# Sliding-window halo by VectorE, dilated v by a casting load: one change to an attention and feed-forward kernel

## The chip, the cores and the metric

The kernel runs on one core of a Trainium2 chip. The metric is the device time in microseconds (us), and less is better. The kernel before takes 308.5 us, the median of three runs (307.8 to 308.51). The profile comes from one further execution, with a span of 307.1 us.

Names used below: PE is TensorE (matrix multiplies), PEld its weight loads, DVE is VectorE, ACT is ScalarE, POOL is GpSimd, SP is SyncE, which here only issues DMA transfers. `Lnnn` is a line of the kernel file.

## The reference

The attention output is laid out token by token and goes through a feed-forward part with a squared ReLU.

```python
# q, k, v: (8 rows of the batch, 8 heads, 576 tokens, 64), float32
window, dilation = 32, 4
rel = pos[:, None] - pos[None, :]
mask_plain = (rel >= 0) & (rel < window)                                        # heads 0 to 3: sliding
mask_dil = (rel >= 0) & (rel < window * dilation) & (rel % dilation == 0)       # heads 4 to 7: dilated
scores = where(mask, q @ k.T / sqrt(64), -1e9)
attn_out = softmax(scores) @ v

x = attn_out.transpose(0, 2, 1, 3).reshape(4608, 512)
out = square(relu(x @ w_in)) @ w_out          # w_in (512, 2048), w_out (2048, 512)
```

## The kernel before

The program goes through the eight batch rows. In row b it issues the attention of row b and, between its pieces, the matmuls of feed-forward chunk b - 1 (512 tokens). The call `pump(n)` issues the next n pieces of that chunk, so that PE always has matmuls between the attention's steps. [...]

For the sliding heads the 576 tokens are cut into six blocks of 96 queries. A block needs the 32 keys before it too, so each block of `vp` has 128 partitions: partitions 32 to 127 hold the block's own 96 tokens, and partitions 0 to 31 the last 32 of the block before. The copy of those 32 partitions (the halo) is what `halo_sliding_by_dma` does. Dilated v has a halo of the same kind, 64 partitions of `vd`.

```python
QB = 96; NB = S // QB; PADP = P - QB          # 96, 6, 32
vp = [const.tile([P, NB, HH, D + 2], FP16, name=f"vp{r}") for r in range(2)]
vd = [const.tile([P, 2, DIL, HH, D + 2], FP16, name=f"vd{r}") for r in range(2)]
sv = stg.tile([P, HH, NB, D], FP32, name="sv")          # staging of sliding v
sd = stg.tile([P, 2, HH, DIL * D], FP32, name="sd")     # staging of dilated v
# ...
def load_sliding_qk(b):                                  # casting loads, issued by GpSimd
    n = natp.tile([P, HH, 9 * D], FP16, name=f"ns{b}", tag="n")
    for i, s in ((1, k), (0, q)):
        nc.gpsimd.dma_start(out=n[64 * i : 64 * (i + 1)], in_=s[b, 0:HH].rearrange(...))
    return n

def load_dilated_v(b, eng):
    vv = v[b, HH:H].rearrange("h (i c) d -> i h (c d)", c=DIL)
    for t in range(2):
        eng.dma_start(out=sd[P - QD[t] : P, t, :, :], in_=vv[Q0D[t] : Q0D[t] + QD[t]])

def cast_sliding_v(b, ms=range(0, NB, 2)):               # 3 casts on GpSimd
    for m in ms:
        nc.gpsimd.tensor_copy(vp[b % 2][:, m : m + 2, :, 0:D], sv[:, :, m : m + 2, :].rearrange(...))

def cast_dilated_v(b):                                   # 4 casts on GpSimd
    for t in range(2):
        p0 = 64 * t
        for c in range(0, DIL, 2):
            nc.gpsimd.tensor_copy(vd[b % 2][p0:P, t, c : c + 2, :, 0:D], sd[p0:P, t, :, D * c : D * (c + 2)].rearrange(...))

def halo_sliding_by_dma(b):
    nc.sync.dma_start(out=vp[b % 2][0:PADP, 1:NB], in_=vp[b % 2][P - PADP : P, 0 : NB - 1])

def halo_dilated_by_dma(b):
    nc.sync.dma_start(out=vd[b % 2][0:64, 1], in_=vd[b % 2][64:P, 0])
# ...
def after_transposes(b):          # GpSimd waits here until the transposes of row b have landed
    nc.gpsimd.tensor_copy(seen, QKTd[b % 2][:, 0, 1, KPAD : KPAD + 1])
# ...
def attn_values_by_dma(b, then):
    xs = x_tiles(b)
    for mp in range(3):
        av_sliding(b, mp, xs)     # matmuls of pav from vp, then rcp_p and xs on VectorE
        if mp == 1:
            then[0]()
        pump(3)
    x_sliding_by_dma(b, xs)       # xT <- xs, DMA transposes
    ys = []
    for t in range(2):
        for a in range(2):
            av_dilated(b, t, a, xs)            # matmuls of paw from vd, then rcp_d and xd on VectorE
            pump(4 + 2 * (a > t))
        ys.append(x_dilated_by_dma(b, t, xs))  # yd <- xd, DMA transpose
        then[1 + t](ys[t])
    pump(6)
    x_from(b, 0, ys[0])                        # xT <- yd on ScalarE
    pump(7)
    x_from(b, 1, ys[1])
# ...
for b in range(4, B):
    pending.append(moe_gen(b - 1))
    nxt = b + 1
    if nxt < B:
        after_transposes(b)
        ns = load_sliding_qk(nxt)
        dd = keep_dilated_qk(nxt)              # q and k of the dilated heads to DRAM as fp16, by GpSimd
    if b > 4:
        cast_dilated_v(b)
    halo_sliding_by_dma(b)
    halo_dilated_by_dma(b)
    dps = []

    def copied():
        if nxt < B:
            dps.append(turn(nxt, ns))          # nr <- ns on VectorE (token order), dp <- nr by SyncE
    def first(y):
        if nxt < B:
            load_sliding_v(nxt)
    def second(y):
        if nxt < B:
            transpose_sliding(nxt, dps[0])     # QKTp <- dp
            transpose_dilated(nxt, dd)         # QKTd <- dd
            load_dilated_v(nxt, nc.sync)       # sd <- v
            nc.gpsimd.tensor_copy(seen, y[:, 0, 0, 0:1])
            cast_sliding_v(nxt)

    pump(3)
    attn_scores(b, 3)
    attn_values_by_dma(b, (copied, first, second))
    pump(1000)
```

The feed-forward chunk ends with seven block products; near the end, `pa` holds the sixth product, `pb` the seventh, and VectorE adds them to the output tiles `ou` and `ov`:

```python
        yield from product(A, sq(1), wq(1, 1))
        take(upper, 1)                                   # ScalarE copies pa
        leave(upper, 0, (1,) if last else (0, 1))        # output store
        yield
        yield from product(Bk, gq(1, 1), tq(3))
        add(o21, Bk)                                     # VectorE: ov
```

Of the kernel before, what the change touches and what calls it, by code (L numbers as in the profile page):

```python
# [8 lines left out]
FP16 = mybir.dt.float16  # L9
# [4 lines left out]
P = 128  # L14
# [3 lines left out]
def kernel(  # L18
# [9 lines left out]
    nc = tc.nc  # L28

    B, H, S, D = q.shape  # L30
    W = 32
    DIL = 4
# [3 lines left out]
    HH = H // 2  # L36
# [10 lines left out]
    NB = S // QB  # L47
    PADP = P - QB
# [41 lines left out]
    vp = [const.tile([P, NB, HH, D + 2], FP16, name=f"vp{r}") for r in range(2)]  # L90
    vd = [const.tile([P, 2, DIL, HH, D + 2], FP16, name=f"vd{r}") for r in range(2)]
    sv = stg.tile([P, HH, NB, D], FP32, name="sv")
    sd = stg.tile([P, 2, HH, DIL * D], FP32, name="sd")
    ident = const.tile([P, P], FP16, name="ident")
    maskp = const.tile([P, UW], FP16, name="maskp")
    maskd = const.tile([P, UW], FP16, name="maskd")
# [12 lines left out]
    def load_sliding_qk(b):  # L109
        n = natp.tile([P, HH, 9 * D], FP16, name=f"ns{b}", tag="n")  # L110
        for i, s in ((1, k), (0, q)):
            nc.gpsimd.dma_start(
                out=n[64 * i : 64 * (i + 1)],
                in_=s[b, 0:HH].rearrange("h (p j) d -> p h (j d)", j=9),
            )
        return n
# [14 lines left out]
            for h in (0, 2):  # L131
                nc.sync.dma_start(out=sv[PADP:P, h : h + 2], in_=vv[:, h : h + 2])  # L132

    def load_dilated_v(b, eng):
        vv = v[b, HH:H].rearrange("h (i c) d -> i h (c d)", c=DIL)
        for t in range(2):
            eng.dma_start(out=sd[P - QD[t] : P, t, :, :], in_=vv[Q0D[t] : Q0D[t] + QD[t]])  # L137
# [29 lines left out]
    def cast_sliding_v(b, ms=range(0, NB, 2)):  # L167
        for m in ms:
            nc.gpsimd.tensor_copy(  # L169
                vp[b % 2][:, m : m + 2, :, 0:D], sv[:, :, m : m + 2, :].rearrange("p h m d -> p m h d")  # L170
            )

    def cast_dilated_v(b):
        for t in range(2):
            p0 = 64 * t
            for c in range(0, DIL, 2):
                nc.gpsimd.tensor_copy(  # L177
                    vd[b % 2][p0:P, t, c : c + 2, :, 0:D],
                    sd[p0:P, t, :, D * c : D * (c + 2)].rearrange("p h (c d) -> p c h d", d=D),
                )  # L180
# [7 lines left out]
    def halo_dilated(b, c):  # L188
        nc.scalar.copy(
            vd[b % 2][0:64, 1, c : c + 2, :, 0:D], vd[b % 2][64:P, 0, c : c + 2, :, 0:D]  # L190
        )

    def halo_sliding_by_dma(b):
        nc.sync.dma_start(out=vp[b % 2][0:PADP, 1:NB], in_=vp[b % 2][P - PADP : P, 0 : NB - 1])
# [9 lines left out]
    def keep_dilated_qk(b):  # L204
        d = dpool.tile([2, HH * CL, DIL * D], FP16, name=f"dd{b}", tag="dd")
        for i, src in ((1, k), (0, q)):
            nc.gpsimd.dma_start(
                out=d[i].rearrange("(r i) x -> r (i x)", i=4),
                in_=src[b, HH:H].rearrange("h (r i) d -> (h r) (i d)", i=16),
                max_dma_last_dim=4096,  # L210
            )
        return d
# [21 lines left out]
    def after_transposes(b):  # L234
        nc.gpsimd.tensor_copy(seen, QKTd[b % 2][:, 0, 1, KPAD : KPAD + 1])
# [117 lines left out]
    def mm2_strassen_gen(c, g):  # L353
        A, Bk, Ck = "abc"
        banks = {}

        def wq(r, q):
            return lambda k: wo[2 * r + k // 4][:, k % 4, HM * q : HM * (q + 1)]

        def gq(i, r):  # L360
            return lambda k, t: g[:, HF * r + k, HTOK * i + P * t : HTOK * i + P * (t + 1)]

        def tq(n):
            return lambda k: wt[n][:, k]

        def sq(n):
            return lambda k, t: gs[n][:, k, P * t : P * (t + 1)]

        def product(bank, a, b, ts=(0, 1)):
            new = bank not in banks  # L370
            if new:
                banks[bank] = pmool.tile([P, 2, HM], FP32, name=f"p{bank}{c}", tag="pm")
            for t in ts:
                for k in range(HF):
                    nc.tensor.matmul(  # L375
                        banks[bank][:, t],
                        a(k, t),
                        b(k),
                        start=(new and t == 0 and k == 0),
                        stop=(k == HF - 1),  # L380
                        skip_group_check=True,
                    )
                    if k % 4 == 3 and (t, k) != (ts[-1], HF - 1):
                        yield

        def half(i):
            return otp.tile([P, 2, DM], FP32, name=f"o{i}_{c}", tag="ot")

        def take(o, j):
            ot = o[:, :, HM * j : HM * (j + 1)]  # L390
            nc.scalar.copy(ot, banks[A])  # L391
            return ot

        def leave(o, i, js):
            t0 = c * TOKC + HTOK * i
            m = slice(HM * js[0], HM * (js[-1] + 1))
            nc.sync.dma_start(
                out=out[t0 : t0 + HTOK, m].rearrange("(t p) m -> p t m", p=P), in_=o[:, :, m]
            )

        def add(ot, bank):
            nc.vector.tensor_add(ot, banks[bank], ot)  # L402

        last = c == NTOKC - 1

        nc.vector.tensor_sub(g[:, 0:HF, HTOK:], g[:, 0:HF, 0:HTOK], g[:, 0:HF, HTOK:])
        yield from product(A, gq(0, 0), wq(0, 0))
        upper = half("u")
        o11 = take(upper, 0)
        yield  # L410
        yield from product(Ck, gq(0, 1), wq(1, 0), (0,))
        yield
        yield from product(A, sq(1), tq(1))
        lower = half("v")
        o21 = take(lower, 0)
        yield
        yield from product(Bk, gq(1, 0), tq(2))
        nc.vector.tensor_sub(gs[1], g[:, HF:, 0:HTOK], gs[1])
        yield
        yield from product(A, sq(0), tq(0))  # L420
        o22 = take(lower, 1)
        add(o22, Bk)
        if last:
            leave(lower, 1, (1,))
        yield
        yield from product(Ck, gq(0, 1), wq(1, 0), (1,))
        add(o11, Ck)
        if last:
            leave(upper, 0, (0,))
        yield  # L430
        yield from product(A, sq(1), wq(1, 1))
        take(upper, 1)
        leave(upper, 0, (1,) if last else (0, 1))
        yield
        yield from product(Bk, gq(1, 1), tq(3))
        add(o21, Bk)
        leave(lower, 1, (0,) if last else (0, 1))
        yield
# [73 lines left out]
    def pump(n):  # L512
        for _ in range(n):
            while pending:
                try:
                    next(pending[0])
                    break
                except StopIteration:
                    pending.pop(0)
# [92 lines left out]
    def x_tiles(b):  # L612
        x = xp.tile([QB, 2, NB, 2, D], FP16, name=f"xs{b}", tag="xs")
        return x, [xp.tile([QD[t], DIL, HH, D], FP16, name=f"xd{b}_{t}", tag=f"xd{t}") for t in range(2)]
# [122 lines left out]
    def attn_values_by_dma(b, then):  # L737
        xs = x_tiles(b)
        for mp in range(3):
            av_sliding(b, mp, xs)  # L740
            if mp == 1:
                then[0]()
            pump(3)
        x_sliding_by_dma(b, xs)
# [3 lines that stand above are left out]
                av_dilated(b, t, a, xs)  # L748
                pump(4 + 2 * (a > t))
            ys.append(x_dilated_by_dma(b, t, xs))  # L750
            then[1 + t](ys[t])
        pump(6)
        x_from(b, 0, ys[0])
        pump(7)
        x_from(b, 1, ys[1])
# [86 lines left out]
    for b in range(2, 4):  # L842
        pending.append(moe_gen(b - 1))
        nxt = b + 1
# [22 lines left out]
# [3 lines that stand above are left out]
        if nxt < B:  # L870
            after_transposes(b)
            ns = load_sliding_qk(nxt)
            dd = keep_dilated_qk(nxt)
        if b > 4:
            cast_dilated_v(b)
        halo_sliding_by_dma(b)
        halo_dilated_by_dma(b)
        dps = []

        def copied():  # L880
            if nxt < B:
                dps.append(turn(nxt, ns))
# [6 lines that stand above are left out]
            if nxt < B:  # L889
                transpose_sliding(nxt, dps[0])  # L890
                transpose_dilated(nxt, dd)
                load_dilated_v(nxt, nc.sync)
                nc.gpsimd.tensor_copy(seen, y[:, 0, 0, 0:1])
                cast_sliding_v(nxt)

        pump(3)
        attn_scores(b, 3)
        attn_values_by_dma(b, (copied, first, second))
        pump(1000)
# [33 lines left out]
```

## Time and profile before

| engine | busy us | share of the span | instructions |
|---|---|---|---|
| PE | 286.5 | 93% | 2762 |
| VectorE | 210.1 | 68% | 434 |
| ScalarE | 172.9 | 56% | 293 |
| GpSimd | 64.2 | 21% | 112 |

Busy time is the time in which an engine executes; issuing DMA transfers isn't counted in it. The PE clock was granted in full over the whole span. The DMA transfers moved 47.03 MB; the queue that SyncE issues to took 51.9% of sixteen DMA engines' span, and the one of GpSimd 26.1%.

| DMA transfer | queue | median us from issue to landing |
|---|---|---|
| `ns` from k, from q | GpSimd | 6.3, 7.8 |
| `dd` from k, from q | GpSimd | 7.1, 8.3 |
| `sd` (dilated v), 320 and 256 KB | SyncE | 6.2, 6.0 |
| `sv` (sliding v), two of 288 KB | SyncE | 5.3 |
| `vp` from `vp` (halo) | SyncE | 5.5 |
| `vd` from `vd` (halo) | SyncE | 6.1 |
| `QKTp` from `dp`, `QKTd` from `dd` | SyncE | 4.9, 4.0 |

A row of the batch is recognised in the timeline by its attention steps: `ps` and `pz` (scores), `pav` (sliding values), `paw` (dilated values). A line of the waits names the engine and line that waited, what released it, the total in us, how many times, and the longest. In the timeline a bracket at the end of a line gives the idle time before the instruction and its releaser.

### The profile page before, as it was taken

What the parts mean: (1) busy time and instruction counts of PE and PEld (TensorE: products, weight loads), DVE (VectorE), ACT (ScalarE), POOL (GpSimd) and SP (SyncE); (2) the same over time, 40 slices, a digit from 0 to 9 for tenths busy, and PEclk for the clock granted to TensorE, in tenths of its full rate; (3) what the DMA queues carried; (4) which work ended last, traced back from release to release, by engine and by line L of the source; (5) the groups of instructions that cost most, each with busy time, mean ns of one, the idle gap of its engine ahead of it and who ended that gap; (6) DMA issues with size and microseconds to landing.
All of it is one profiled execution on the core that took longest, in us unless ns stands there. A gap on an engine that the chain in (4) does not pass through costs nothing.

```text
span 307.1 us, 6899 instructions
## 1 busy us (share of the span) xinstructions
PE 286.5 (93%) x2762; PEld 192.4 (63%) x2762; DVE 210.1 (68%) x434; ACT 172.9 (56%) x293; POOL 64.2 (21%) x112
## 2 busy tenths in 40 slices
PE   1788998999999899999998999799989999999994
PEld 1345554555554468656887987458745875785584
DVE  7684447758843798489759984999398934834652
ACT  2766648668745863595457636763486446425620
POOL 4481027002704503310027002700230000000000
PEclk9999999999999999999999999999999999999999
DMA  7899998799599999995799979997983231003004
GB/s 116 187 204 213 208 173 152 157 215 221 119 211 176 242 191 187 258 187 120 127 171 260 220 126 188 267 189 131 158 252 22 45 111 40 2 1 139 0 1 138
DMA packets 77616, 47.03 MB, mean 153 GB/s; under 512 B 58480, under 2 KB 69232, under 8 KB 77584
## 3 DMA queue, kind: packets, MB, share of 16 engines
q1 hardware_dynamic: 68832, 32.96, 51.9%
q0 software_dynamic: 8752, 13.63, 26.1%
q8 instruction: 21, 0.34, 0.5%
q14 instruction: 11, 0.09, 0.1%
HBM read 36.70 MB, written 16.52 MB: 173 GB/s over the span
## 4 chain that ended last, share of the span: by engine, by line
PE 72%; DMA 12%; DVE 6%; SPq 3%; ACT 3%; issue 2%; POOL 0%; DVEq 0%; POOLq 0%
PE ph L298 32%; PE pa L375 15%; PE pb L375 7%; DMA vp<-vp 6%; PE po L441 6%; DMA QKTp<-dp 4%; PE pc L375 4%; PE paw L638 2%; PE pav L622 2%; DMA QKTd<-dd 1%; PE ps L573 1%; DMA sv<-in_v_dram 1%; ACT AT L563 1%; SPq L137 1%; SPq L132 1%
## 5 line engine op out<-in xcount | busy, mean ns | idle before, releaser
L298 PE MATMUL ph<-xT,wi 128*128 128x512 f16 (+1 forms) x640 | 134.2, 359 | 0.7 <-ACT xT L675 0.7
L321 ACT ACTIVATE rt<-ph 128x512 f16<-128x512 f32 x144 | 86.2, 608 | 47.5 <-PE ph L298 46.4
L298 PEld LDWEIGHTS <-wi 128*128 128x128 f16 x640 | 68.2, 114 | 45.9 <-issue 0.6
L322 DVE TENSOR_TENSOR g<-rt 128x512 f16<-128x512 f16 x144 | 63.4, 450 | 39.6 <-ACT rt L321 38.1
L375 PEld LDWEIGHTS <-g 128*128 128x128 f16 x448 | 43.3, 98 | 6.1
L375 PEld LDWEIGHTS <-gs 128*128 128x128 f16 x336 | 32.1, 98 | 4.0 <-DVE gs L332 0.3
L441 PE MATMUL po<-wo,g 128*128 128x512 f16 x128 | 33.1, 379 | 0.0
L402 DVE TENSOR_TENSOR ov<-pb,ov 128x512 f32<-128x512 f32 x14 | 9.7, 691 | 30.8 <-PE pb L375 17.4
L375 PE MATMUL pa<-wt,gs 128*128 128x256 f16 x224 | 27.2, 273 | 0.0
L375 PE MATMUL pb<-wt,g 128*128 128x256 f16 x224 | 27.1, 273 | 0.0
L169 POOL CAST vp<-sv 128x512 f16<-128x512 f32 x24 | 15.2, 664 | 53.4 <-DMA sv<-in_v_dram 39.5
L391 ACT COPY ov<-pa 128x512 f32<-128x512 f32 x14 | 8.2, 586 | 30.7 <-PE pa L375 30.7
L177 POOL CAST vd<-sd 128x512 f16<-128x512 f32 (+1 forms) x32 | 22.1, 717 | 11.4 <-PE ph L298 8.0
L610 DVE TENSOR_TENSOR xd<-paw,rcp_d 80x512 f16<-80x512 f32 (+1 forms) x32 | 21.9, 685 | 1.1
L563 ACT ACTIVATE AT<-pz 128x576 f16<-128x576 f32 x32 | 19.7, 694 | 1.2 <-PE pz L592 1.1
L563 ACT ACTIVATE AT<-ps 128x576 f16<-128x576 f32 x32 | 19.2, 657 | 2.2 <-PE ps L573 1.8
L564 DVE TENSOR_TENSOR AT<-AT,maskd 128x576 f16<-128x576 f16 x32 | 18.4, 604 | 1.8 <-ACT AT L563 0.7
L564 DVE TENSOR_TENSOR AT<-AT,maskp 128x576 f16<-128x576 f16 x32 | 15.5, 492 | 5.9 <-ACT AT L563 4.2
L391 ACT COPY ou<-pa 128x512 f32<-128x512 f32 x14 | 8.2, 586 | 15.8 <-PE pa L375 15.7
L610 DVE TENSOR_TENSOR xs<-pav,rcp_p 96x512 f16<-96x512 f32 x24 | 16.5, 687 | 0.8
L622 PEld LDWEIGHTS <-AT 128*128 128x128 f16 x192 | 9.3, 98 | 10.8 <-issue 6.0
L441 PEld LDWEIGHTS <-g 128*128 128x128 f16 x128 | 10.4, 98 | 8.3
(80 smaller groups left out, 276.7 us busy)
## 6 DMA issues: line engine op xcount, KB each, us to landing
sv<-in_v_dram SPq DMA_DIRECT2D x14, 288.0 KB, 5.3
dp<-nr SPq DMA_DIRECT2D x12, 288.0 KB, 4.0
out_dram<-ou SPq DMA_DIRECT2D x6, 512.0 KB, 4.0
out_dram<-ov SPq DMA_DIRECT2D x6, 512.0 KB, 4.7
sd<-in_v_dram SPq DMA_DIRECT2D x8, 320.0 KB, 6.2
ns<-in_k_dram POOLq DMA_DIRECT2D x8, 288.0 KB, 6.3
ns<-in_q_dram POOLq DMA_DIRECT2D x8, 288.0 KB, 7.8
sd<-in_v_dram SPq DMA_DIRECT2D x8, 256.0 KB, 6.0
```

The costliest lines, as they stand in the source:

```text
L169: nc.gpsimd.tensor_copy(vp[b % 2][:, m : m + 2, :, 0:D], sv[:, :, m : m + 2, :].rearrange("p h m d -> p m h d"))
L177: nc.gpsimd.tensor_copy(vd[b % 2][p0:P, t, c : c + 2, :, 0:D], sd[p0:P, t, :, D * c : D * (c + 2)].rearrange("p h (c d) -> p c h d", d=D),)
L298: nc.tensor.matmul(ph[:, t0:t1], wi4[ffc // 4][:, dmk, :, ffc % 4], xT[:, dmk, x0 : x0 + t1 - t0], start=(dmk == 0 and t0 == 0), stop=(dmk ...
L321: nc.scalar.activation(rt, ph[:], ACTF.Relu)
L322: nc.vector.tensor_mul(g[:, ffc, :], rt, rt)
L375: nc.tensor.matmul(banks[bank][:, t], a(k, t), b(k), start=(new and t == 0 and k == 0), stop=(k == HF - 1), skip_group_check=True,)
L391: nc.scalar.copy(ot, banks[A])
L441: nc.tensor.matmul(po, g[:, ffc, t * P : (t + 1) * P], wo[ffc // 4][:, ffc % 4, :], start=(ffc == 0), stop=(ffc == NFF - 1),)
L563: nc.scalar.activation(AT[:, u, 0:UW], ps[:, :, 0 : UW // 2], ACTF.Exp, scale=scale)
L564: nc.vector.tensor_mul(AT[:, u, 0:UW], AT[:, u, 0:UW], mask)
L610: nc.vector.tensor_tensor(out=x, in0=pv, in1=rb, op=ALU.mult)
L622: nc.tensor.matmul(pav[:, i, h * (D + 2) : h * (D + 2) + D + 1], AT[:, 2 * (h // 2) + m // 3, off : off + P], vp[b % 2][:, m, h, 0 : D + 1 ...
```

## The change

It touches rows 5 to 7 of the batch, in four ways.

- The halo of sliding v is copied by VectorE at the end of the chunk before, after the sliding casts of the next row, and no longer by a DMA at the start of the row. It is meant to take that DMA's landing out of the path to the first `pav` matmuls.
- Dilated v is loaded at the start of its own row by GpSimd, with the cast to fp16 in the load, between the loads of sliding and of dilated q and k. Before, SyncE loaded it as fp32 at the end of the row before. The fp16 data lie in the first half of the same staging tile, and GpSimd then copies them into `vd` as before, from fp16.
- The token-order copy `nr` comes after the third sliding tile in place of the second.
- SyncE's queue thus loses two loads and one halo copy per row.

```diff
+    sd16 = sd.rearrange("p t h x -> p (t h x)")[:, 0 : HH * DIL * D].bitcast(FP16)
+    sd16 = sd16.rearrange("p (t h x) -> p t h x", t=2, h=HH)
 ...
-    def load_dilated_v(b, eng):
+    def load_dilated_v(b, eng, sd=sd):
 ...
-    def cast_dilated_v(b):
+    def cast_dilated_v(b, sd=sd):
 ...
+    at_end: list = []
+
+    def halo_sliding_at_end(b):
+        nc.vector.tensor_copy(
+            vp[b % 2][0:PADP, 1:NB, :, 0:D], vp[b % 2][P - PADP : P, 0 : NB - 1, :, 0:D]
+        )
 ...
         leave(upper, 0, (1,) if last else (0, 1))
+        while at_end:
+            at_end.pop()()
         yield
         yield from product(Bk, gq(1, 1), tq(3))
 ...
-            if mp == 1:
+            if mp == (2 if b > 4 else 1):
                 then[0]()
 ...
             ns = load_sliding_qk(nxt)
+        if b > 4:
+            load_dilated_v(b, nc.gpsimd, sd16)
+        if nxt < B:
             dd = keep_dilated_qk(nxt)
         if b > 4:
-            cast_dilated_v(b)
-        halo_sliding_by_dma(b)
+            cast_dilated_v(b, sd16)
+        else:
+            halo_sliding_by_dma(b)
         halo_dilated_by_dma(b)
 ...
                 transpose_sliding(nxt, dps[0])
                 transpose_dilated(nxt, dd)
-                load_dilated_v(nxt, nc.sync)
                 nc.gpsimd.tensor_copy(seen, y[:, 0, 0, 0:1])
                 cast_sliding_v(nxt)
+                at_end.append(lambda: halo_sliding_at_end(nxt))
```

## The prediction

> **What bounds the kernel now.** I read the page first. TensorE (PE) is busy 93% of the 307.1 us span at full granted clock, so time can only come from places where PE stands still. The chain of work that ended last shows which waits those are:
>
> ```profile
> PE 72%; DMA 12%; DVE 6%; SPq 3%; ACT 3%; issue 2%; POOL 0%; DVEq 0%; POOLq 0%
> PE ph L298 32%; PE pa L375 15%; PE pb L375 7%; DMA vp<-vp 6%; PE po L441 6%; DMA QKTp<-dp 4%; PE pc L375 4%; PE paw L638 2%; PE pav L622 2%; DMA QKTd<-dd 1%; PE ps L573 1%; DMA sv<-in_v_dram 1%; ACT AT L563 1%; SPq L137 1%; SPq L132 1%
> ```
>
> `vp<-vp`, the halo copy of sliding v by DMA, is 6% of the chain. Nothing like that can be saved, because PE works during most of it. So I took the chain in order of time (start, duration, what), and then the waits between 150 and 255 us (total, times, longest), which count only what PE lost:
>
> ```profile
> 161.55 5.53 DMA vp<-vp
> 191.85 6.88 DMA vp<-vp
> 216.18 5.38 DMA QKTp<-dp
> 224.17 5.56 DMA vp<-vp
> ```
>
> ```profile
> PE pav L622 <- DMA vp<-vp: 3.8, 3, 1.6
> ```
>
> Three copies, one in each of rows 5, 6 and 7, and 3.8 us of waiting in all. In the timeline of row 5 it looks like this:
>
> ```profile
> 158.93 1.37 SPq L137 DMA_DIRECT2D sd<-in_v_dram  x2
> 161.55 0.72 SPq L194 DMA_DIRECT2D vp<-vp  x1
> 164.14 2.98 POOL L177 CAST vd<-sd 128x512 f16<-128x512 f32 x4
> 165.54 0.29 PE L622 MATMUL pav<-vp,AT 128*128 128x65 f16 x4
> 167.12 0.29 PE L622 MATMUL pav<-vp,AT 128*128 128x65 f16 x4 [1.29 <-DMA vp<-vp]
> ```
>
> The first four `pav` matmuls (block 0) need no halo; the next four wait 1.29 us. The copy is issued only at 161.55 because the SyncE queue is in order and first issues the `sd` loads of dilated v and two output stores.
>
> A second measure includes the restart. The first hidden-layer matmul of each row starts at 127.27, 157.04, 188.44, 220.00 and 251.00 us in the timeline, so rows 4 to 7 last 29.77, 31.40, 31.56 and 31.00. Row 4 does the same matmul work, has the halo by DMA too, but early (landed 3.3 us after its issue at 128.68), and waits for nothing. Rows 5 to 7 lie 1.63, 1.79 and 1.23 above it. **4.65 us (1.5%) is the whole prize**: the time cannot well go under 308.5 - 4.65 = 303.85.
>
> [...] `nr` (2304 fp16 elements per partition) takes 0.751 us, 3.07 elements per ns. [...] the mask multiply averages 0.458 us in row 4's first stage, where GpSimd casts nothing, and 0.718, 0.706 and 0.647 in rows 5 to 7, where the `vd` casts run; the `g` multiply 0.425 against 0.538. [...]
>
> **The change part by part.**
>
> 1. Halo of sliding v by VectorE. Removed: three `vp<-vp` copies, hence 3.8 us of PE waits. Added: three copies of 5 x 4 x 64 = 1280 elements at the `nr` rate, 1280 / 3.07 = 0.42 us each. They stand behind the sum `ou` and ahead of `ov`, at the tail of the chunk before. In row 5's tail the `vp` casts end at 185.89 + 1.72 = 187.61, and VectorE waits for PE until 188.64; 187.7 + 0.42 fits. Rows 4 and 6 are alike (casts end 155.35 and 218.16, VectorE idle until 157.24 and 220.20). Cost zero, gain up to 4.65.
>
> 2. Dilated v by a casting load at the start of rows 5 to 7. Before, it was loaded by SyncE at 158.93 and its casts were done at 167.1, 4.5 us before use. Now, in row 5: the guard on `QKTd` passes at 161.5, `ns` k and q are issued at 161.79 and 162.43 (0.65 and 0.62 us each), the two `sd16` loads at about 163.0 and 163.6. They follow `ns` through the same queue. `ns` q landed 8.2 us after issue in row 5 and 6.8 in row 4, where less ran beside it. With the `sd` load (576 KB) and the `vp` copy gone and the stores 1.5 us earlier my estimate is 7, so 169.3. In row 4 `dd` (576 KB) came 2.9 us after `ns` (136.75 to 139.6), so half as many bytes, the two `sd16` pieces, take about 1.5: 170.0 for the first, 170.8 for the second. The first cast ends near 170.8. In row 4 the first `paw` matmul comes 13.07 us after the row's start; in row 5 that is 157.04 + 13.07 = 170.11. So **a new wait of about 0.7 us**. For the lower half, two casts must end (171.5) and the halo copy `vd<-vd` must land: 2.6 us in the quiet row 7, 6.1 to 6.5 in the busy rows 5 and 6. My estimate lies between, 4.3: 175.8, against a need at 17.91 after the start plus 0.7 = 175.65. About 0.2 more. Row 6: its `ns` is issued 3.93 us after the row's start, not 4.75, so all comes 0.8 sooner: near zero wait, 0.1. Row 7 has no q and k to load, and its load can go out at the end of row 6, so no wait.
>
> 3. The `vd` casts move from 164 to 167 us, where VectorE catches up during the PE wait, to 170 to 173. From there VectorE is busy without a gap: 1.93 to 1.97 of every 2 us between 172 and 182. Their lock-out costs VectorE seven slow `g` (0.11 each) and four mask multiplies (0.25 each), some 1.8 us; my estimate is that 0.8 of it stays in the new place. It delays the last `xd`, the second `yd` transpose, and then `QKTp<-dp` behind it in the SyncE queue, which row 7 already waits for slightly (landed 221.56, first `ps` at 221.60; 0.15 us of PE idle). Row 6 has about 0.3 us of slack (second issue 184.69, landing 4.8 us later at 189.5; `ps` at 189.83). So 0.5 lost at the start of row 6 and 0.8 at row 7's. At the end of row 6 the early `sd16` load also runs beside these transposes: 0.2 more.
>
> 4. `nr` one tile later, in rows 5 and 6: `ns` lands before VectorE comes to it. It is for this that it is there; `dp`, 12 us ahead of the transposes that read it, has slack. The store of `dp` goes ahead of the `xT` transposes in SyncE's queue, about 1.5 us later than now; in row 4's times SyncE would still be free 0.6 us before the second `yd` transpose needs it. Zero.
>
> Sum: -4.65 + 0.9 (row 5) + 0.1 (row 6) + 0.5 + 0.8 + 0.2 = **-2.15, that is 306.3 us**.
>
> **The rivals.** (a) The full prize: casting loads land early, and nothing replaces the wait: 303.9. For it: the DMA engines have less to do (the windows' DMA share is above 1.0 from 160 to 174 us, and 288 KB of fp16 replaces 576 KB of fp32 plus the halo). Against it: the cast and the halo copy of dilated v come after the landing now. (b) a wait for `vd` takes the place of `pav <- vp` in rows 5 and 6: if `sd16` lands as late as `dd` does now (10.4 us after issue, 174), the waits are near 4 to 5 us each and the time is 311 or more. Against it: `sd16` stands ahead of `dd` in the queue. (c) `QKTp<-dp` becomes the bound, because VectorE's backlog and SyncE's order carry over from row to row: rows 6 and 7 lose what they gain, 307.5. (d) Nothing moves: all three replaced by other waits, 308.5.
>
> **Range and chances.** The floor is (a), the upper end a half-strength (b) with (c): 304.2 to 308.8. Faster by over 2% would need 302.3, below the floor; slower by over 2% needs 314.7, twice (b).
>
> **What would show it.** Right: no `pav <- vp` wait; rows 5 to 7 of about 30.7, 30.3 and 30.8 us; a short `paw <- vd` (GpSimd or DMA) wait in row 5; halo copies on VectorE of 0.4 us in its idle time; slow VectorE multiplies at 170 to 173; `ps <- QKTp` waits of up to 1 us at the starts of rows 6 and 7. Wrong: rows of 29.8 (I overrated 2 and 3), or a `paw` wait over 2 us a row (I underrated the load's landing), or VectorE standing at the halo copy because the sliding casts come late, which would hold up the next chunk.

## The result, and the profile after

The changed kernel takes 306.13 us (median of four executions, 305.54 to 306.23) against 308.5 us before. The ratio is 0.992, with a 95% interval of 0.990 to 0.994: faster by 2.4 us, or 0.8%. The forecast was 306.3 us in a range of 304.2 to 308.8. Not all of that need be the change's doing. The spans of the two profiled executions differ by 2.8 us; 1.96 of that lies in rows 5 to 7 (table below) and 0.95 ahead of row 4, where nothing was changed (row 4 starts at 127.27 us before and at 126.32 after).

The first view is the chain of work that ended last, from the page of the changed kernel, by engine and by line:

```profile
PE 78%; DVE 11%; DMA 5%; ACT 3%; issue 1%; SPq 0%; POOL 0%; DVEq 0%; POOLq 0%
PE ph L307 36%; PE pa L384 14%; PE po L452 8%; PE pb L384 8%; PE pc L384 3%; DMA sd<-in_v_dram 3%; DVE g L331 3%; PE ps L584 2%; PE paw L649 2%; DMA QKTp<-dp 2%; PE pz L603 1%; DVE xd L621 1%; DVE gs L340 1%; PE pav L633 1%; ACT AT L574 1%
```

`vp<-vp` (6% before) is gone from it, and DMA fell from 12% to 5%. In its place VectorE (DVE) rose from 6% to 11%. The waits between 150 and 255 us (total in us, times, longest) say where PE and VectorE stood still:

```profile
DVE vp L198 <- POOL vp L171: 3.5, 3, 1.6
...
PE pa L384 <- DVE gs L341: 0.8, 2, 0.5
...
PE ps L584 <- DMA QKTp<-dp: 0.7, 1, 0.7
```

There is no wait of PE for `vp` any more (3.8 us before), and none for `vd`. There is a new one for `gs`, an operand that VectorE makes for the second `pa` product of a feed-forward chunk. In row 5 the sum that PE waits for is this line, first in the kernel before and then in the changed one:

```profile
178.51 0.69 DVE L332 TENSOR_TENSOR gs<-gs,g 128x1024 f16<-128x1024 f16 x1
```

```profile
177.35 0.69 DVE L341 TENSOR_TENSOR gs<-gs,g 128x1024 f16<-128x1024 f16 x1
```

Counted from the start of the row (157.04 and 156.09) it ends at 22.2 us before and at 21.9 after; in row 4, where PE waits for nothing, it ends at 20.5. So VectorE is no later with it than it was. PE used to come to this product late itself, at 21.8 us, because it had stood for `vp`; now it comes at 21.0.

The first line of the waits is VectorE standing at the new halo copy until the sliding casts are done. The prediction named this as a sign of being wrong, if it held up the next chunk. No wait of PE follows from it: it happens at the end of a row, where VectorE waited before too (for `pb`, 9.8 us before and 4.9 after). Row 5 in the timeline of the changed kernel:

```profile
162.12 1.29 POOL L139 DMA_DIRECT2D sd<-in_v_dram  x2
...
165.31 0.42 PE L633 MATMUL pav<-vp,AT 128*128 128x65 f16 x8
...
168.09 3.76 POOL L179 COPY vd<-sd 128x512 f16<-128x512 f16 x4 [3.58 <-PE pav L633]
...
170.01 0.42 PE L649 MATMUL paw<-vd,AT 128*128 128x65 f16 x8
...
186.66 0.48 DVE L198 COPY vp<-vp 32x1280 f16<-32x1280 f16 x1 [1.64 <-POOL vp L171]
```

All eight `pav` matmuls now run in one piece. The casting loads of dilated v are issued at 162.12, GpSimd begins to copy from them at 168.09, and the first `paw` at 170.01 does not wait.

The table has the length of rows 5 to 7, from the first hidden-layer matmul of a row to that of the next, in the profiled execution of each kernel below. Row 4 takes 29.77 or 29.78 us in every one of them. Times and ratios stand beside executions of the kernel before on the same chip. That kernel's median was 309.1, 310.9 and 309.3 us in the three sets of runs, so across sets only ratios are compared. Medians and ratios leave out executions more than 1.5% above the fastest of the same kernel. Single executions scatter by several us. The row lengths are the finer instrument, but they come from one execution, and not always from a typical one: it was the slowest of its kernel for the halo by VectorE alone (307.85 us) and for the second of the changed kernel (307.97), and the fastest for the halo by DMA (304.82), for the load at the row's end (303.85) and for the third of the changed kernel (305.51).

| kernel | us | ratio to before (95% interval) | row 5 | row 6 | row 7 |
|---|---|---|---|---|---|
| before | 308.5 | 1 | 31.40 | 31.56 | 31.00 |
| changed | 306.13 | 0.992 (0.990 to 0.994) | 31.19 | 30.85 | 29.96 |
| set 1: halo by VectorE alone | 306.32 | 0.990 (0.987 to 0.993) | 31.81 | 31.92 | 29.78 |
| set 1: changed, halo by DMA | 307.16 | 0.994 (0.991 to 0.997) | 30.93 | 30.74 | 29.77 |
| set 1: changed, no `vd` copies in rows 5, 6 | 304.96 | 0.987 (0.982 to 0.991) | 30.33 | 29.78 | 29.82 |
| set 1: load at the row's end, copies in the tail | 306.59 | 0.989 (0.982 to 0.996) | 29.94 | 30.01 | 30.39 |
| set 2: changed, again | 307.65 | 0.983 (0.974 to 0.993) | 31.29 | 30.30 | 31.29 |
| set 2: changed, `nr` early | 307.27 | 0.985 (0.976 to 0.995) | 30.97 | 30.88 | 30.01 |
| set 2: load a row ahead | 304.48 | 0.975 (0.969 to 0.982) | 29.94 | 29.78 | 29.86 |
| set 2: before, order of two transfers | 307.67 | 0.987 (0.978 to 0.996) | 30.58 | 31.12 | 29.78 |
| set 3: changed, third time | 306.44 | 0.993 (0.990 to 0.996) | 31.05 | 30.84 | 29.94 |
| set 3: load a row ahead, again | 304.70 | 0.983 (0.980 to 0.987) | 29.94 | 29.78 | 29.77 |
| set 3: load a row ahead, halo by DMA | 304.31 | 0.982 (0.978 to 0.985) | 29.93 | 29.78 | 29.77 |

### The profile page after: what moved, and what is told of

It is laid out like the page before. It is cut to its first block, busy times and chain, and to the rows that moved or that the text cites. A ratio compares the mean times of both kernels' runs of the same rounds, so it can differ in the third digit from the quotient of the medians.

```text
span 304.3 us, 6891 instructions
## 1 busy us (share of the span) xinstructions
PE 288.3 (95%) x2762; PEld 193.2 (63%) x2762; DVE 209.7 (69%) x437; ACT 173.2 (57%) x293; POOL 69.4 (23%) x118
## 4 chain that ended last, share of the span: by engine, by line
PE 78%; DVE 11%; DMA 5%; ACT 3%; issue 1%; SPq 0%; POOL 0%; DVEq 0%; POOLq 0%
PE ph L307 36%; PE pa L384 14%; PE po L452 8%; PE pb L384 8%; PE pc L384 3%; DMA sd<-in_v_dram 3%; DVE g L331 3%; PE ps L584 2%; PE paw L649 2%; DMA QKTp<-dp 2%; PE pz L603 1%; DVE xd L621 1%; DVE gs L340 1%; PE pav L633 1%; ACT AT L574 1%
## 5 line engine op out<-in xcount | busy, mean ns | idle before, releaser
L411 DVE TENSOR_TENSOR ov<-pb,ov 128x512 f32<-128x512 f32 x14 | 9.7, 692 | 25.8 <-ACT ov L400 13.2
L171 POOL CAST vp<-sv 128x512 f16<-128x512 f32 x24 | 14.5, 633 | 52.3 <-DMA sv<-in_v_dram 52.3
L621 DVE TENSOR_TENSOR xd<-paw,rcp_d 80x512 f16<-80x512 f32 (+1 forms) x32 | 21.9, 684 | 1.1
L575 DVE TENSOR_TENSOR AT<-AT,maskp 128x576 f16<-128x576 f16 x32 | 16.2, 517 | 5.9 <-ACT AT L574 4.2
L575 DVE TENSOR_TENSOR AT<-AT,maskd 128x576 f16<-128x576 f16 x32 | 15.6, 504 | 2.4 <-ACT AT L574 0.9
L649 PEld LDWEIGHTS <-AT 128*128 128x128 f16 x256 | 12.0, 98 | 5.8 <-PE px L662 1.0
L179 POOL CAST vd<-sd 128x512 f16<-128x512 f32 (+1 forms) x20 | 13.3, 692 | 7.4 <-DMA sd<-in_v_dram 7.2
```

Source lines behind the costliest of these rows:

```text
L575: nc.vector.tensor_mul(AT[:, u, 0:UW], AT[:, u, 0:UW], mask)
L621: nc.vector.tensor_tensor(out=x, in0=pv, in1=rb, op=ALU.mult)
L649: nc.tensor.matmul(pav[:, e, h * (D + 2) : h * (D + 2) + D + 1], AT[:, 4 + h, off : off + P], vd[b % 2][:, t, 2 * a + e, h, 0 : D + 1], st ...
```

## The experiments

Two questions were open. Which of the four parts took the wait for `vp` away? And what is it that still makes rows 5 and 6 about 1.1 to 1.4 us longer than row 4? Where the recorded texts speak of a lock-out of VectorE, the traces show longer VectorE instructions beside GpSimd's casts and copies: in row 6 of the changed kernel two `g` take 1.58 us with copies beside them and 0.75 without.

### The halo by VectorE alone

The changed kernel with dilated v by SyncE as before and `nr` after the second tile, so that only the VectorE halo copy is left of the change.

```diff
-            if mp == (2 if b > 4 else 1):
+            if mp == 1:
 ...
-        if b > 4:
-            load_dilated_v(b, nc.gpsimd, sd16)
 ...
-            cast_dilated_v(b, sd16)
+            cast_dilated_v(b)
 ...
                 transpose_dilated(nxt, dd)
+                load_dilated_v(nxt, nc.sync)
```

> Part 1 alone: VectorE copies the sliding halo, dilated v comes by SyncE as fp32 and is cast early in the row as before, nr after the second sliding tile. Theory A (what is left in rows 5 and 6 of the changed kernel, about 1.1 us a row, is the late vd copies on GpSimd locking VectorE out at 12 to 16 us after the row's start, until a Strassen product waits for gs): the casts lie at 7 to 10 us again, VectorE has time to recover, rows 5 and 6 take about 30.0 us and the time is about 304.5. Rival B (the lock-out costs the same wherever it falls before gs): rows of about 30.8, time about 306. Rival C (nr stalls VectorE when it comes before the q and k loads have landed): rows 5 and 6 above 31, a wait of VectorE ahead of nr, time 306.5 or more.

It took 306.32 us, and rows 5 and 6 were the longest of all the kernels, 31.81 and 31.92. Its waits between 150 and 255 us:

```profile
DVE nr L122 <- DMA ns<-in_q_dram: 1.2, 1, 1.2
...
PE ps L584 <- DMA QKTp<-dp: 1.0, 1, 1.0
PE paw L649 <- DVE xs L621: 1.0, 1, 1.0
PE pa L384 <- DVE gs L341: 1.0, 2, 0.5
```

Theory A, that casts early in the row leave VectorE time to recover, fell: the casts run from 163.42 and 194.36 us, 7 us into the row, and PE still waits for `gs` in both rows. B fits: with the casts early, VectorE is still late with `gs`. How much of a row's length is due to the casts alone can't be read here, because each row has a second disturbance. In row 6 it is C: `nr` stood 1.2 us for the load of q, and PE then waited 1.0 us for VectorE. In row 5 the `QKTp` transposes landed 1.0 us late (below). The median of 306.32 us is what B expected; the rows come from the slowest execution.

### The changed kernel with the halo by DMA again

```diff
             cast_dilated_v(b, sd16)
-        else:
-            halo_sliding_by_dma(b)
+        halo_sliding_by_dma(b)
 ...
-                at_end.append(lambda: halo_sliding_at_end(nxt))
```

> The changed kernel with the halo of sliding v by DMA at the row's start again (part 1 undone). If the wait for vp came only from the SyncE queue being held by the two sd loads and so late an issue, the copy now goes out some 2 us earlier, lands before the first pav, and the time stays at about 306. If its landing beside the q and k loads is what is slow (5.5 to 6.9 us before), it lands 0.5 to 1 us late in rows 5 and 6, and the time is about 307 to 307.5.

In the trace PE does not wait for `vp`. The copies are issued at 157.51, 188.29 and 219.32 us, 2.3 to 2.6 us after the rows' starts (4.5, 3.4 and 4.2 before the change), and they land 4.3 to 5.3 us later, ahead of the first `pav` at 8.4. The rows are no longer than those of the changed kernel. The time, 307.16 us, is spread over 304.82 to 308.87, and its interval overlaps that of the changed kernel, so it settles nothing. This trace also shows what a wait for `gs` costs: in row 6 PE waits for nothing else, 0.48 us, and the row is 0.97 longer than row 4. The trace says that the VectorE copy isn't needed once SyncE's queue is free of the two loads.

### The kernel before with two transfers in another order

To see whether the place in the queue is enough by itself, the kernel before got one edit:

```diff
+        halo_sliding_by_dma(b)
         if b > 4:
+            load_dilated_v(b, nc.sync)
             cast_dilated_v(b)
-        halo_sliding_by_dma(b)
 ...
-                load_dilated_v(nxt, nc.sync)
```

> The kernel before with one thing changed: SyncE issues the two fp32 loads of dilated v after the halo copy of sliding v and not ahead of it (nothing by VectorE, no casting load, nr where it was). Theory Q (the wait for vp came from the halo copy's late issue behind these loads): the copy goes out 2.5 us earlier, and the wait of PE for vp, 3.8 us before, falls below 0.5. Rival (the copy is slow because of the loads that run beside it, wherever it stands): a wait of 0.5 to 1 us a row stays. The time under Q is about 306.5, since the casts into vd come late and lock VectorE out at 11 to 15 us, and nr may wait for its loads; under the rival about 308.

Q holds. Its timeline in row 5, where the fp32 loads still run at the same time, but behind the halo:

```profile
159.42 1.27 SPq L194 DMA_DIRECT2D vp<-vp  x1
160.74 1.96 SPq L137 DMA_DIRECT2D sd<-in_v_dram  x2
...
165.53 0.42 PE L622 MATMUL pav<-vp,AT 128*128 128x65 f16 x8
...
178.44 1.48 PE L375 MATMUL pa<-wt,gs 128*128 128x256 f16 x12 [0.47 <-DVE gs L332]
```

The copy goes out 2.1 us earlier, `pav` runs in one piece, and no wait for `vp` is left in any row. An earlier issue is not the whole of it, though. In row 6 the copy is issued 2.5 us after the row's start and not 3.4, only 0.9 earlier, and it lands sooner after its issue (the kernel before, then this one):

```profile
DMA to landing us min/median/max: 6.9/6.9/6.9
```

```profile
DMA to landing us min/median/max: 5.2/5.2/5.2
```

So the edit helps in two ways, by an earlier issue and by a faster landing, and in row 6 the second is the larger (1.7 us). For that part the rival, that the copy is slow because of what runs beside it, is not ruled out. In place of the wait for `vp` comes the same wait for `gs` as in the changed kernel (0.47 us here). So reordering two transfers brings about what the whole change brought: a ratio of 0.987 beside 0.983 for the changed kernel in the same set, with intervals that overlap.

### The changed kernel without the copies into `vd`

In rows 5 and 6 GpSimd's copies from `sd16` into `vd` are left out, so these rows use the dilated v of rows 3 and 4. The loads and all other work stay.

```diff
         if b > 4:
-            cast_dilated_v(b, sd16)
+            if b == 7:
+                cast_dilated_v(b, sd16)
         else:
             halo_sliding_by_dma(b)
```

> The changed kernel without GpSimd's copies into vd in rows 5 and 6 (these rows then use the dilated v of rows 3 and 4; everything else stays, loads included). Theory A (lock-out of VectorE by these copies): the waits of PE for gs vanish, nr and g run at full speed in rows 5 and 6, rows of about 29.8 to 30.0, time about 304.4. Rival (the rest comes from the q and k loads, the transposes or nr itself): no change, 306.

Row 6 fell from 30.85 to 29.78, which is row 4's length, and the waits for `gs` are gone; the time is 304.96 us. Row 6 of the changed kernel, as the timeline has it (four copies on GpSimd, and beside them `nr`, two `g` and the first sum `gs`):

```profile
199.52 3.64 POOL L179 COPY vd<-sd 128x512 f16<-128x512 f16 x4 [4.46 <-DMA sd<-in_v_dram]
...
200.44 0.74 DVE L122 COPY nr<-ns 128x2304 f16<-128x2304 f16 x1
...
201.10 1.58 DVE L331 TENSOR_TENSOR g<-rt 128x512 f16<-128x512 f16 x2
...
202.71 0.99 DVE L340 TENSOR_TENSOR gs<-g 128x1024 f16<-128x1024 f16 x1
...
208.20 0.69 DVE L341 TENSOR_TENSOR gs<-gs,g 128x1024 f16<-128x1024 f16 x1
...
208.95 1.48 PE L384 MATMUL pa<-wt,gs 128*128 128x256 f16 x12 [0.48 <-DVE gs L341]
```

And without the copies:

```profile
199.86 0.75 DVE L122 COPY nr<-ns 128x2304 f16<-128x2304 f16 x1
200.52 0.75 DVE L331 TENSOR_TENSOR g<-rt 128x512 f16<-128x512 f16 x2
201.31 0.69 DVE L340 TENSOR_TENSOR gs<-g 128x1024 f16<-128x1024 f16 x1
...
206.50 0.69 DVE L341 TENSOR_TENSOR gs<-gs,g 128x1024 f16<-128x1024 f16 x1
...
206.87 1.91 PE L384 MATMUL pa<-wt,gs 128*128 128x256 f16 x16
```

Two `g` take 1.58 us beside the copies and 0.75 without, the first `gs` 0.99 and 0.69. The sixteen matmuls of the product run in one piece, where in the changed kernel they were cut into 4 and 12 by the wait. Counted from the row's start (187.28 and 186.70), the sum that PE waits for ends at 21.61 us with the copies and at 20.49 without, 1.12 apart, and row 6 is 1.07 shorter. What held row 6, and about 0.5 us of row 5, is thus the longer VectorE instructions beside GpSimd's copies, and the delay reaches PE through the operand `gs`. The 0.55 us that row 5 still has is a late start, 0.4 (its first `ps` comes 1.80 us after the row's start, not 1.41, for `QKTp`), and 0.15 that it has in every kernel: it runs 128 hidden-layer matmuls of half width where rows 4, 6 and 7 run 64, and row 5 is never under 29.93 in the table.

### `nr` after the second tile again

```diff
-            if mp == (2 if b > 4 else 1):
+            if mp == 1:
```

> The changed kernel with nr after the second sliding tile again (part 4 undone). Theory N (the q and k loads land only about then, and VectorE stands in front of nr): in rows 5 and 6 nr comes 1.5 us earlier, VectorE waits 0.3 to 1 us for ns, and since it has no slack before the product that reads gs, each of the two rows gets that much longer, together 0.5 to 1.5 us, time about 307. Rival (the loads now land some 2 us earlier than before the change, at about 10.5 us after the row's start, and nr comes at 12): no wait for ns, time the same within 0.3 us.

The rival holds. There is no wait for `ns`; rows 5 and 6 take 30.97 and 30.88, those of the changed kernel in the same set 31.29 and 30.30, and the times are 307.27 and 307.65 us with overlapping intervals. With dilated v in GpSimd's queue `ns` lands 4.5 to 5.8 us after its issue in row 5 (7.4 to 8.2 before), and so `nr` would not wait even where it was. In the first experiment, with the fp32 loads by SyncE and `nr` early, it waited 1.2 us in row 6. The third part may thus matter together with those loads; no run had them with `nr` late.

### Dilated v earlier, copies in the tail

If this slowing of VectorE is all that is left, the copies into `vd` belong where VectorE is idle, at the end of the row. First version: the casting load is issued when the first `yd` transpose of the row before has landed, and the copies follow the sliding casts.

```diff
 (in first)
+                nc.gpsimd.tensor_copy(seen, y[:, 0, 0, 0:1])
+                load_dilated_v(nxt, nc.gpsimd, sd16)
 (in second)
                 cast_sliding_v(nxt)
+                cast_dilated_v(nxt, sd16)
 (at the row's start)
-        if b > 4:
-            load_dilated_v(b, nc.gpsimd, sd16)
 ...
-            cast_dilated_v(b, sd16)
```

> The changed kernel with the casting load of dilated v issued in the row before, after the first yd transpose has landed, and the copies into vd right after the sliding casts, in the tail of that row, where VectorE is idle. Theory A: nothing locks VectorE out in the middle of rows 5 and 6, all three rows take about 29.8 to 30.0 us, time about 304.0, ahead of both kernels. Rival D (the load beside the transposes of q and k makes them land late): waits of PE for QKTp or QKTd of about 0.5 to 1 us at the starts of rows 5 to 7, time about 305.5 to 306.

The slowing is gone: in rows 5 and 6 the two `g` behind `nr` take 0.75 us and the first `gs` 0.69, and there is no wait for `gs`. But rows 6 and 7 now start with waits for `QKTp` of 0.7 us together, as rival D has it. The time is inconclusive, with a spread of 303.85 to 307.18 us.

Second version: the load goes out a row ahead, behind the loads of dilated q and k, so that it does not run beside those transposes.

```diff
             dd = keep_dilated_qk(nxt)
+            load_dilated_v(nxt, nc.gpsimd, sd16)
 ...
                 cast_sliding_v(nxt)
+                cast_dilated_v(nxt, sd16)
 (the load and the copies at the row's start are taken out as above)
```

> The changed kernel with the casting load of dilated v a whole row ahead, in GpSimd's queue right behind the loads of dilated q and k, and the copies into vd in the tail of that row after the sliding casts. Theory A (lock-out of VectorE in mid-row is all that is left) and no other transfer beside the transposes of q and k at the row's end: rows 5 to 7 of 29.8 to 30.0 us, no waits for gs, none for QKTp beyond 0.3, time about 303.5 to 304.5. Rival: the load delays dp and the xT transposes, and the transposes of q and k still come late; waits for QKTp of 0.5 us or more, 305 to 306.

Rows of 29.94, 29.78 and 29.86: nothing is left of the prize. Its time was 304.48 us. The changed kernel, which ran beside it, had 307.65:

> The changed kernel once more, unaltered, as the yardstick for the other three. Every theory expects 0.992 of the kernel before, and rows 5 to 7 of about 30.5 to 31.2, 30.8 and 29.9 us; what differs from the first profile in these rows is how much one execution differs from another.

Its ratio, 0.983 (0.974 to 0.993), lies lower than the 0.992 expected; the kernel before scattered widely in this set (310.3 to 313.6 us). Row 7 was longer than expected, 31.29 (below). So both were run again in a third set, with more executions:

> The changed kernel unaltered, as the yardstick beside the two kernels that load dilated v a row ahead. Expected 0.985 to 0.993 of the kernel before; rows 5 to 7 together 1.5 to 3 us above three times 29.78.

> The kernel with the casting load of dilated v a row ahead and the copies into vd in the tail, again. If its lead is real, it comes out at 0.975 to 0.985 of the kernel before and 2 to 3 us under the changed kernel on the same chip, with rows 5 to 7 within 0.3 us of 29.8; if the first result was a matter of that chip, less than 1 us under it.

The row-ahead kernel came to 304.70 us against 306.44, ratios of 0.983 (0.980 to 0.987) and 0.993 (0.990 to 0.996), which do not overlap. The lead of 1.7 us is below the 2 to 3 expected, and the rows are as expected. The tail of row 5 in this run:

```profile
183.82 1.72 POOL L171 CAST vp<-sv 128x512 f16<-128x512 f32 x3
185.50 2.66 POOL L179 COPY vd<-sd 128x512 f16<-128x512 f16 x4
185.57 0.87 DVE L198 COPY vp<-vp 32x1280 f16<-32x1280 f16 x1 [1.41 <-POOL vp L171]
...
192.19 1.34 POOL L139 DMA_DIRECT2D sd<-in_v_dram  x2
```

The four copies take 2.66 us here and took 3.64 in mid-row. They hold up the halo copy on VectorE (0.87 in place of 0.48 us), and are longer beside it: in the first run of this kernel, of seven at the ends of rows 4 and 5, the longest takes 0.88 us and the median 0.62. Neither does harm there. The load at 192.19 is the one for row 7.

Last, the same kernel with the sliding halo by DMA:

```diff
-        if b == 4:
-            halo_sliding_by_dma(b)
+        halo_sliding_by_dma(b)
 ...
-                at_end.append(lambda: halo_sliding_at_end(nxt))
```

> The same, with the halo of sliding v by DMA at the row's start and not by VectorE. If the wait for vp was all the place in SyncE's queue, it does not come back (the copy goes out about 2 us after the row's start and lands by 7, ahead of the first pav at 8.4), and the time is that of the kernel with VectorE's halo within 0.5 us. If VectorE's copy is what took it away, waits for vp of 0.5 us or more in rows 5 and 6 come back, and the time is 1 us longer or more.

```profile
188.21 1.00 SPq L203 DMA_DIRECT2D vp<-vp  x1
...
194.74 0.42 PE L633 MATMUL pav<-vp,AT 128*128 128x65 f16 x8
```

The copy is issued 1.9 us after the row's start at 186.32 and landed 5.8 us later, at 194.0, 0.7 us ahead of the first `pav`. At 304.31 us it is as fast as the one with VectorE's copy; the first part of the change is not needed.

### What differs between executions of the same kernel

The changed kernel has three profiled executions. Row 5 started with a wait for `QKTp` in each (its first `ps` came 2.13, 2.09 and 1.78 us after the row's start, and 1.39 to 1.41 in an undisturbed row), and row 7 took 29.96, 31.29 and 29.94 us. This is row 7 of the second:

```profile
218.66 1.43 POOL L139 DMA_DIRECT2D sd<-in_v_dram  x2
...
220.72 0.43 PE L584 MATMUL ps<-QKTp 64*128 64x96 f16 x12 [0.61 <-DMA QKTp<-dp]
...
225.10 0.44 PE L603 MATMUL pz<-QKTd 64*128 64x80 f16 x16 [0.76 <-DMA QKTd<-dd]
```

Here the load for row 7 is issued beside the transposes of q and k, and both land late. But the kernels with the halo by DMA and without the copies have the same load at the end of row 6, issued 1.9 and 1.8 us before row 7's start (1.0, 0.0 and 0.9 in the changed kernel), and rows of 29.77 and 29.82. Whether the load delays the transposes is therefore left open. So is the late start of row 5. Six profiled executions end row 4 with the halo by VectorE and no copies into `vd` behind the casts (the three of the changed kernel, halo alone, no copies, `nr` early), and row 5 starts late in all but the last, by 0.4 to 1.1 us. In the four with the halo by DMA it never does. No run tests whether the copy on VectorE has a part in this. The row-ahead kernels, which have no load there, showed no wait for `QKTp` in rows 5 and 6 in three executions, and in row 7 the first `ps` at most 0.09 us late.

## Why the prediction was right

The time lies 0.2 us from the forecast. The sum of what rows 5 to 7 keep above row 4 was forecast as 0.9 + 0.1 + 0.5 + 0.8 + 0.2 = 2.5 us and measured as 1.42 + 1.08 + 0.19 = 2.69. That the two are so close is luck. Row by row the forecast was 0.9, 0.6 and 1.0, so it was 0.5 too low in rows 5 and 6 and 0.8 too high in row 7. What was right is that the wait for `vp` goes, that VectorE's longer instructions beside GpSimd's copies take back a part of it, and that the rest is gained.

- **The prize** of 4.65 us, from row 4's length: right. The row-ahead kernels reach 29.77 to 29.94 in all three rows, and in the third set they are 4.6 and 5.0 us faster than the kernel before.
- **Step 1, the halo on VectorE**: the wait for `vp` is gone and the copy costs nothing on the path; 0.48 us against 0.42 forecast. The credit was misplaced, though. The prediction said that the copy waits in SyncE's queue behind the `sd` loads, and did not draw the conclusion that moving these loads is enough. Three kernels show that it is (the two with the halo by DMA, and the reordering).
- **Step 2, a new wait for `vd`** of 0.7 + 0.2 us in row 5 and 0.1 in row 6: did not come. The mis-sized terms are landings. For `ns` q 7 us was assumed, and 13.0 us after the row's start for the first piece of `sd16` (170.0). The landing of `ns` in row 5, in the kernel before and in the changed one:

```profile
DMA to landing us min/median/max: 7.4/7.8/8.2
```

```profile
DMA to landing us min/median/max: 4.7/5.1/5.5
```

The first piece of `sd16`, issued at 162.12, landed 5.9 us later, 11.9 after the row's start, and the halo copy of dilated v took 3.1 and 2.2 us in rows 5 and 6 where 4.3 was assumed. The late start of row 5 isn't what hid the wait: with the halo by DMA row 5 starts on time and its first `paw` comes at 13.2 us, as in the row-ahead kernels. The slow landings of before go with SyncE's fp32 loads: the kernel with the halo by VectorE alone, which keeps them, has 7.4 to 8.2 too, and the kernels without them 4.5 to 6.7 in row 5. The output stores behind those loads may have a part in it (last section).

- **Step 3, the lock-out of VectorE**: that VectorE's instructions are longer while GpSimd's copies run is right (two `g` 1.58 us against 0.75), and the size is near (1.3 us forecast, about 1.6 measured), but the path by which the delay reaches PE is not. It was to travel over the last `xd`, the `yd` transpose and `QKTp` to the starts of rows 6 and 7 (0.5 + 0.8). In the first profile the first `ps` of both came at 1.39 us, undisturbed. It travels over `gs`, in the row itself, to the second `pa` product: about 0.5 us in row 5 and 1.1 in row 6. The other 0.7 of row 5 is a late `QKTp` at its own start, which no term of the sum had. The prediction saw VectorE busy without a gap from 172 to 182 us, and `gs` in that stretch, but did not ask which of its results PE needs first.
- **The load beside the transposes**, 0.2 us: row 7 kept 0.19 in the first profile, 0.16 in the third, 1.51 in the second; the mechanism is open.
- **Step 4, `nr` one tile later**: costs nothing, as forecast, but it doesn't bring anything in the changed kernel either.

Of the rivals, (a) is what the row-ahead kernels are; (b) did not happen, and (c), `QKTp` as the bound of rows 6 and 7, not in the first profile; row 7 of the second has a wait of that kind, 0.61 us.

## What to carry to other kernels

Before a transfer that is waited for is moved to another engine, look at what stands ahead of it in its queue and at what runs beside it: here a reordering of two transfers took the same wait away. When a wait that gave a busy engine time to catch up is removed, look for the first result of that engine that the next stage reads: here the next wait stood there (`gs`, about 0.5 us). Work that slows another engine belonged, here, in that engine's idle stretch, even though its input then had to be loaded a whole row ahead.

## What the runs showed of the hardware

GpSimd's copy from fp16 was no cheaper than its cast from fp32, twice the source bytes at the same element count. In the row-ahead kernel with the halo by DMA, where VectorE has no copy beside them, the last three of the four copies at the end of row 5 take 1.84 us together, about 0.61 each, and each of the three sliding casts ahead of them takes 0.60 to 0.61. In mid-row the four copies of row 5 or 6 took 3.76 and 3.64 us in the first profile of the changed kernel. Nor is it always VectorE's instruction that is longer: in row 5 of the changed kernel one copy took 1.90 us, while `nr` beside it kept the 0.75 us that it takes without the copies.

The other surprise is how much `ns` gained from its new neighbours: in row 5 it lands some 2.5 us sooner with 288 KB of casting load queued behind it than with 576 KB of plain fp32 loads from SyncE's queue. Part of that may belong to two output stores of 512 KB each. They stood behind the fp32 loads and landed up to 9.9 us after the row's start, beside `ns`; now they have landed by 6.8. In the kernel with two transfers in another order the stores are early (6.6) and the fp32 loads still there, and `ns` lands 6.1 to 7.5 us after issue, in between.
